# Talking-heads attention with a squared-ReLU MLP on one core: two A v pairs and up to two sets of transposes in every other heavy step

## Chip, cores and metric

One core of one Trainium2 chip runs the whole program. The metric is device time in microseconds (us): the median of three runs of the kernel before was 918.96 us (918.96 to 919.45).

## The reference

The inputs are q, k, v of 4 batches x 12 heads x 448 rows x 64, two 12 x 12 head mixes, and an MLP of 768 x 2048 x 768 over the 1792 rows that attention gives.

```python
scores = scale * np.matmul(q, k.transpose(0, 1, 3, 2))
scores = np.einsum('bhij,hg->bgij', scores, w_pre)
attn = np.exp(scores - np.max(scores, axis=-1, keepdims=True))
attn = attn / (np.sum(attn, axis=-1, keepdims=True) + 1e-09)
attn = np.einsum('bhij,hg->bgij', attn, w_post)
x = np.matmul(attn, v)            # then (B*S, H*D)
h = np.maximum(x @ w_in, 0.0)
out = (s * (h * h) + b) @ w_out
```

## The kernel before

**Tiling.** Each batch's 448 query rows are cut into four chunks of 110, 110, 110 and 118 rows (16 chunks, `chunks`), and each chunk into blocks of up to 10 rows (180 blocks, `blocks`). A block with its 12 heads fills 120 partitions, so a head mix is one matrix product with a 120 x 120 weight. fp32 values are carried as a high part and a remainder ("low part"), and a product is three matmuls: low x high, high x low, high x high.

**Steps.** The loop over `s` is a software pipeline, one block a step. In step s TensorE does `premix(s)` (M: 3 matmuls to `pm`, L612) and `postmix(s-3)` (P: 12 f16 matmuls from `eh` to `po`, L660). VectorE does the row maximum of block s (L619), the reciprocal (L636), the remainder of `eh` of block s-1 (`remainder`, L645) and the copy of `po` into A of block s-4 (`evacuate`, L676). ScalarE does exp (L624) and the f16 high part (`normalize`, L638). GpSimd makes the high and low parts of block s+2 (`split`, L597 and L598), SyncE's queue loads block s+5 from S (`relayout`, L589).

**Work beside the blocks.** Later chunks are prepared in the same steps. Per chunk, `prep_q` makes two sets of transposes of q (4 head pairs and 2 head pairs, L478), `qk_pair` six products q k into a two-bank PSUM tile `sc` (6 matmuls each, L503; ScalarE copies it to S, L513), and `av_pair` six products A v (8 matmuls in the code, 16 rows in the trace, L531). A new batch needs six sets of transposes of k besides (`prep_k`, 4 transposes each, L458). A set lies in a tile of the tag `sc`, of which there is one buffer, and only its first bank is used. ScalarE copies the high part out (L462, L482), and VectorE makes the low part from PSUM and that copy (L239). The low part is put on a list, `later`, and issued by the next `low_parts()`. A q k product behind a set therefore waits for that set's low part twice over: as data or because the tile `sc` must be free.

**What sets the order.** Which step does what is a table, `plan`, made before the loop (L699 to L800): `visits(ci)` names six steps for the q k pairs of a chunk, `prep_q`, `prep_k` and their loads get steps by hand, and the A v pairs get two of the q k steps each. `run_plan(s, True)` issues the loads, `run_plan(s, False)` the rest behind `postmix`. In steps listed in `ahead`, premix, postmix and one set of transposes are issued ahead of the element-wise work. A loop joins two A v pairs into one step only where a transposition stands in the step before (`behind`); elsewhere the pairs stay in steps of their own. In `full` (steps with a q k pair whose predecessor has none) `low_parts()` and `evacuate` come behind the softmax.

**End of attention.** From step 165 (`tail - XA`) on, the first batch's x is split for the MLP: `split_x` has ScalarE copy the high part, and `low_parts` VectorE subtract (L239, both inputs in SBUF), one of six in each of the steps 166 to 171. The MLP's matmuls (L254, L311) follow from about 455 us on.

```python
        low_parts()
        if (s in full or (s >= tail + 4 and s % 2 == 0)) and 0 <= s - 4 < NB:
            evacuate(s - 4)
        if 0 <= s - 1 < NB:
            remainder(s - 1)
        run_plan(s, True)
        if 0 <= s - 3 < NB and s not in ahead:
            postmix(s - 3)
        run_plan(s, False)
```

Of the kernel before, what the change touches and what calls it, by code (L numbers as in the profile page):

```python
# [21 lines left out]
def talking_heads_attention__then__act_relu2_kernel(  # L22
# [427 lines left out]

    def prep_k(b, p):
        low_parts()
        nat = nat_t.pop((b, p))
        tr = bank(f"trk_{b}_{p}") if b == 0 else ps.tile([P, 2, 512], F32, tag="sc", name=f"trk_{b}_{p}")[:, 0]

        for c in (NC - 1, *range(NC - 1)):
            j0 = c * P if b == 0 else min(c * P, S - P)
            nc.tensor.transpose(  # L458
                tr[:, j0:j0 + P], nat[:, c].rearrange("p h d -> p (h d)"), ident
            )  # L460
        t = qkp.tile([P, 2, S], F32R, tag="Tk", name=f"Tk_{b}_{p}", bufs=8)
        nc.scalar.activation(t[:, 0, :], tr[:, :S], AF.Copy)  # L462
        later.append((t[:, 1, :], tr[:, :S], t[:, 0, :]))
        k_t[b, p] = t

    def prep_q(ci, half):

        b, n0, n = chunks[ci]
        low_parts()
# [5 lines left out]
        tr = bank(f"trq_{ci}_{ps_[0]}") if ci < 2 else ps.tile([P, 2, 512], F32, tag="sc", name=f"trq_{ci}_{half}")[:, 0]  # L475
# [226 lines left out]
    fill = []  # L702
    for ci in range(2, NCH):
        b, _, _ = chunks[ci]
        w0 = first[ci - 1] - LD
        news = chunks[ci - 1][0] != b
        back = w0 - (first[ci - 2] - LD)
        if news:
            starts = (w0 - back + 6, w0 - back + 2)
        else:  # L710
            starts = (w0 - back + (10 if back == 12 else 8), w0 + 4)
        for half, step in enumerate(starts):
            at(step, 1, prep_q, ci, half)
            load[step] = 0.375
        if ci > 2:
            at(min(starts) - 8, 0, load_q, ci)
        for p, step in enumerate(visits(ci)):
            if news:
                t = w0 - back + 8 if p == 0 else w0 + 2 * p - 2
                at(t, 1, prep_k, b, p)  # L720
                load[t] = 0.6
                at(t - 4, 0, load_k, b, p)
            at(step, 3, qk_pair, ci, p)
            load[step] = load.get(step, 0) + QK_COST
    ahead = {}
    for ci in range(NCH):
        b = chunks[ci][0]
        w0 = first[ci + 1] + 4
        if ci < NCH - 2:
# [3 lines left out]
            behind = {x[0] + 1 for x in plan if x[3] in (prep_q, prep_k)}  # L733
            for i in range(0, NP, 2):
                if steps[i] not in behind or steps[i + 1] not in behind:
                    j = i if steps[i] in behind or steps[i + 1] not in behind else i + 1
                    steps[i] = steps[i + 1] = steps[j]
                    for n, x in enumerate(plan):
                        if x[0] == steps[j] - 1 and x[3] in (prep_q, prep_k):
                            plan[n] = (-1, *x[1:])  # L740
                            ahead[steps[j]] = x[3:]
# [49 lines left out]
    plan = [x for x in plan if x[0] >= 0]  # L791
# [77 lines left out]
    for s in range(NB + 4):  # L869
# [16 lines left out]
        if 0 <= s - 1 < NB:  # L886
            ops = 7 * NU_EARLY
            due = ops * (s - CONV0) / (tail - LD - 2 * NP - CONV0)
            if s - 1 in mixes:
                for spare in (0, 2):  # L890
                    if turn["ops"] + spare < due:
                        turn["ops"] += convert_step(NU_EARLY)
            if s in ahead:
                premix(s)
                postmix(s - 3)
                f, args = ahead[s]
                f(*args)
            normalize(s - 1)
# [9 lines left out]
        low_parts()  # L908
# [4 lines left out]
        if 0 <= s - 1 < NB:  # L913
            remainder(s - 1)
        run_plan(s, True)
# [124 lines left out]
```

## Time and profile before

| what | value |
|---|---|
| median of three runs | 918.96 us |
| profiled execution: its time, its span | 918.51 us, 916.8 us |
| TensorE busy | 905.5 us (99%) |
| VectorE busy | 652.1 us (71%) |
| ScalarE busy | 562.4 us (61%) |
| GpSimd busy | 394.5 us (43%) |
| mean granted TensorE clock | 0.999 |
| chain that ended last, TensorE's share | 90% |

The profile's page gives busy time by engine (above) and the chain that ended last. The time line of TensorE then gives, from the start of one group of matmuls to the start of the next, what each group costs in its surroundings; a group's own printed length overlaps the next one's, since matmuls are pipelined. The steps can be counted by the premix rows, L612.

### The profile page before, as it was taken

The page shows a single profiled execution, that of the slowest core. Times are in us where ns is not written, and L with a number is a line of the kernel's source. Part 1 is how long each engine was busy: PE and PEld are TensorE (multiplying, and loading weights), DVE is VectorE, ACT ScalarE, POOL GpSimd, SP SyncE. Part 2 cuts the span into 40 slices and gives each one's busy share as a digit, 9 for nine tenths or more (in the row PEclk, how much of TensorE's full clock was granted, in tenths as well). Part 3 has the DMA queues.
Part 4 walks back from the last instruction along what each step waited for, and adds up shares of the span by engine and source line. Part 5 has one row for each costly group of instructions (what it writes and reads, how often), then busy time and mean ns, then how long its engine had stood idle before and what let it go on. Part 6 is the DMA issues. An engine that isn't in the chain of part 4 may idle for free.

```text
span 916.8 us, 19938 instructions
## 1 busy us (share of the span) xinstructions
PE 905.5 (99%) x7538; PEld 784.0 (86%) x7538; DVE 652.1 (71%) x1370; ACT 562.4 (61%) x1260; POOL 394.5 (43%) x454
## 2 busy tenths in 40 slices
PE   8999999999999999999999999999999999999998
PEld 4677777777777777777899999999999999999998
DVE  5889988988989988889796079939107915977111
ACT  5888888888888888887587876021127688600000
POOL 4976677766767677677242333000003333300000
PEclk9999999999999999999999999999999999999999
DMA  5665557564566645546124132344411420345321
GB/s 144 184 158 152 154 136 180 153 158 127 152 162 161 166 127 143 154 131 209 52 68 150 40 95 87 104 156 155 138 44 35 147 78 18 87 155 189 130 95 53
DMA packets 126557, 115.24 MB, mean 126 GB/s; under 512 B 63960, under 2 KB 122348, under 8 KB 126460
## 3 DMA queue, kind: packets, MB, share of 16 engines
q1 hardware_dynamic: 116934, 102.28, 39.7%
q10 hardware_dynamic: 9366, 11.59, 3.5%
q8 instruction: 60, 0.98, 0.4%
q14 instruction: 37, 0.30, 0.1%
q0 software_dynamic: 160, 0.09, 0.1%
HBM read 58.87 MB, written 16.52 MB: 82 GB/s over the span
## 4 chain that ended last, share of the span: by engine, by line
PE 90%; DVE 4%; ACT 3%; DMA 2%; issue 1%; POOL 0%; SPq 0%; ACTq 0%
PE po L311 25%; PE ph L254 24%; PE pm L612 12%; PE po L660 10%; PE xp L531 8%; PE sc L503 7%; DVE st L619 1%; PE ph_head L254 1%; ACT pm L624 1%; PE trk L458 1%; DVE A L676 1%; DMA blk<-S 1%; PE trq L478 1%; ACT S L513 1%; ACT eh L638 1%
## 5 line engine op out<-in xcount | busy, mean ns | idle before, releaser
L311 PE MATMUL po<-w,g 128*128 128x384 f32 x1344 | 233.5, 336 | 0.0
L311 PEld LDWEIGHTS po<-w,g 128*128 128x128 f32 x1344 | 233.0, 188 | 0.3 <-ACT ob L318 0.3
L598 POOL TENSOR_TENSOR hl<-blk,hl 120x448 fp32r<-120x448 f32 (+1 forms) x179 | 204.9, 1145 | 14.9
L272 POOL TENSOR_TENSOR g<-h,g 128x448 fp32r<-128x448 f32 x64 | 79.6, 1244 | 278.9 <-ACT g L271 259.3
L254 PE MATMUL ph<-x,w 128*128 128x448 f32 x810 | 164.1, 362 | 0.0
L254 PEld LDWEIGHTS ph<-x,w 128*128 128x128 f32 x810 | 151.9, 188 | 10.2
L660 PEld LDWEIGHTS <-eh 120*128 120x128 f16 (+1 forms) x2160 | 115.2, 98 | 41.7 <-issue 34.5
L597 POOL TENSOR_SCALAR hl<-blk 120x448 fp32r<-120x448 f32 (+1 forms) x179 | 102.9, 575 | 101.8 <-PE pm L612 93.4
L660 PE MATMUL po<-wpost,eh 120*128 120x120 f16 (+1 forms) x2160 | 144.7, 217 | 0.8 <-DVE A L676 0.4
L645 DVE SCALAR_TENSOR_TENSOR eh<-pm,st,eh 120x448 f16<-120x448 f32 x180 | 122.3, 679 | 18.0 <-ACT eh L638 15.4
L638 ACT ACTIVATE eh<-pm,st 120x448 f16<-120x448 f32 x180 | 114.1, 634 | 14.3 <-DVE st L636 13.8
L619 DVE TENSOR_REDUCE st<-pm 120x1 f32<-120x448 f32 x180 | 110.3, 613 | 11.9 <-PE pm L612 11.1
L624 ACT ACTIVATE pm<-pm,st 120x448 f32<-120x448 f32 x180 | 109.6, 609 | 9.3 <-DVE st L619 7.6
L676 DVE COPY A<-po 128x480 f32<-128x480 f32 x174 | 111.6, 641 | 0.1
L513 ACT ACTIVATE S<-sc 110x896 f32<-110x896 f32 (+1 forms) x91 | 83.5, 917 | 40.2 <-PE sc L503 31.9
L612 PE MATMUL pm<-hl,wpre_hi 120*120 120x448 f32 x360 | 102.4, 366 | 0.7 <-POOL hl L598 0.3
L531 PE MATMUL xp<-A,v 128*64 128x110 f32 (+1 forms) x1536 | 87.1, 263 | 0.0
L503 PE MATMUL sc<-Tk,Tq 64*110 64x448 f32 (+1 forms) x576 | 82.5, 391 | 2.9 <-DVE Tq L239 1.1
L612 PE MATMUL pm<-hl,wpre_lo 120*120 120x448 f32 x180 | 82.8, 460 | 1.6 <-DVE st L636 1.6
L531 PEld LDWEIGHTS xp<-A,v 128*64 128x64 f32 x1536 | 74.0, 137 | 7.3 <-issue 1.3
L318 ACT ACTIVATE ob<-po 128x384 f32<-128x384 f32 x28 | 13.8, 493 | 98.0 <-PE po L311 84.3
L612 PEld LDWEIGHTS pm<-hl,wpre_hi 120*120 120x120 f32 x360 | 64.9, 182 | 6.8 <-POOL hl L598 1.7
(83 smaller groups left out, 970.9 us busy)
## 6 DMA issues: line engine op xcount, KB each, us to landing
blk<-S SPq DMA_DIRECT2D x172, 210.0 KB
raw<-in_moe_w_in_dram SPq DMA_DIRECT2D x32, 384.0 KB
raw<-in_moe_w_out_dram SPq DMA_DIRECT2D x32, 384.0 KB
xraw<-xd SPq DMA_DIRECT2D x48, 224.0 KB
part<-ob ACTq DMA_DIRECT2D x28, 192.0 KB
acc<-part SPq DMA_DIRECT2D x28, 192.0 KB
out_dram<-acc ACTq DMA_DIRECT2D x28, 192.0 KB
v<-in_v_dram SPq DMA_DIRECT2D x24, 192.0 KB
```

Source lines behind the costliest of these rows:

```text
L254: nc.tensor.matmul(ph[:, :S], w[:, i, c0:c0 + P], x[:, y, :], start=(kc == 0 and m == 0), stop=(kc == NKC - 1 and m == 2),)
L311: nc.tensor.matmul(po[:, :NO], g[:, x, c0:c0 + P], w[:, y, :], start=(f == 0 and m == 0), stop=(f == NF - 1 and m == 2),)
L503: nc.tensor.matmul(sc[e][:n, :S], qt[r0:r0 + D, p, x, :n], kt[r0:r0 + D, y, :], start=(m == 0), stop=(m == 2),)
L531: nc.tensor.matmul(xp[e * D:(e + 1) * D, p % 4, :n], vt[:, e, c, :], a[:, c, 2 * p + e, :n], start=(c == 0), stop=(c == NC - 1),)
L598: eng.tensor_tensor(out=hl[:n, 1, :], in0=blk[:n], in1=hl[:n, 0, :].bitcast(F32), op=ALU.subtract)
L612: nc.tensor.matmul(pm[:n, :S], w[:n, :n], hl[:n, x, :], start=(m == 0), stop=(m == 2))
L619: nc.vector.tensor_reduce(out=st[:n, 0:1], in_=pm[:n, :S], axis=AX.X, op=ALU.max, negate=True)
L624: nc.scalar.activation(e[:n], e[:n], AF.Exp, bias=st[:n, 0:1], accum_out=pm[:n, S:S + 1])
L638: nc.scalar.activation(eh[:n, 0, :], e[:n], AF.Copy, scale=st[:n, 3:4])
L645: nc.vector.scalar_tensor_tensor(out=eh[:n, 1, :], in0=e[:n], scalar=st[:n, 3:4], in1=eh[:n, 0, :], op0=ALU.mult, op1=ALU.subtract,)
L660: nc.tensor.matmul(po[:, c * BP:(c + 1) * BP], eh[:n, x, j0:j0 + P], wpost[:n, y].rearrange("p g i -> p (g i)"), start=(m == 0), stop=(m = ...
L676: nc.vector.tensor_copy(dst, src)
```

## The change

In `plan`, for chunks 2 to 15, the A v pairs always come two and two (`steps[p - p % 2]`), and the sets of transposes move to the steps that have them, up to two sets a step (`ahead` now holds a list). The two sets of a step share the two banks of one `sc` tile (`tr_bank`). q k alone stands in the visits between. `prep_k` and `prep_q` of later chunks no longer begin with `low_parts()`. The loads of k keep to 3 to 7 steps ahead of their transposes (before: 4). In the loop, `low_parts()` behind the softmax is kept only up to step 166, and one is added behind `remainder`.

```diff
+    def tr_bank(name):
+        if x_t.get("at") != state["step"]:
+            x_t["at"] = state["step"]
+            x_t["tr"] = ps.tile([P, 2, 512], F32, tag="sc", name=name)
+            return x_t["tr"][:, 0]
+        return x_t["tr"][:, 1]
+
     def prep_k(b, p):
-        low_parts()
+        if b == 0:
+            low_parts()
         nat = nat_t.pop((b, p))
-        tr = bank(f"trk_{b}_{p}") if b == 0 else ps.tile([P, 2, 512], F32, tag="sc", name=f"trk_{b}_{p}")[:, 0]
+        tr = bank(f"trk_{b}_{p}") if b == 0 else tr_bank(f"trk_{b}_{p}")
...
-            steps = [x for x in visits(ci + 2) if x >= w0] + [x for x in after if x < first[ci + 2] + 4]
...
-        news = chunks[ci - 1][0] != b
-        back = w0 - (first[ci - 2] - LD)
...
+        vis = visits(ci)
+        for p, step in enumerate(vis):
             at(step, 3, qk_pair, ci, p)
             load[step] = load.get(step, 0) + QK_COST
-    ahead = {}
+        if ci < 4:
+            for half, step in enumerate(((3, 10), (14, vis[2]))[ci - 2]):
+                if step == vis[2]:
+                    ahead.setdefault(step, []).append((prep_q, (ci, half)))
+                else:
+                    at(step, 1, prep_q, ci, half)
...
+        prev = visits(ci - 1)
+        if chunks[ci - 1][0] != b:
+            when = prev[4], vis[0], vis[0], vis[2], vis[4], vis[4]
+            for p, step in enumerate(when):
+                at((prev[4] - 4, vis[0] - 4, vis[0] - 3, vis[0] - 1, vis[0] + 1, vis[0] + 3)[p], 0, load_k, b, p)
+                ahead.setdefault(step, []).append((prep_k, (b, p)))
+            step = prev[2]
+        elif chunks[ci - 2][0] != b:
+            step = vis[0]
+        else:
+            step = prev[4]
+        ahead.setdefault(step, []).append((prep_q, (ci, 0)))
+        ahead.setdefault(vis[2], []).append((prep_q, (ci, 1)))
+        at(step - 8, 0, load_q, ci)
...
-            behind = {x[0] + 1 for x in plan if x[3] in (prep_q, prep_k)}
-            for i in range(0, NP, 2):
-                if steps[i] not in behind or steps[i + 1] not in behind:
...
+            steps = [steps[p - p % 2] for p in range(NP)]
...
-                f, args = ahead[s]
-                f(*args)
+                for f, args in ahead[s]:
+                    f(*args)
...
-        low_parts()
+        if s <= tail - XA + 1:
+            low_parts()
...
             remainder(s - 1)
+        low_parts()
         run_plan(s, True)
```

TensorE, steps 74 to 76 (the premix `pm` names the step; `trk_2_1` is a set of transposes of k for batch 2, pair 1; `xp` an A v pair, `sc` a q k pair; of the 24 rows of each postmix the first two are shown). Before:

```order
L612 MATMUL pm_74_3581<-hl_74_3491,wpre_hi_125 120x448 x2
...
L531 MATMUL xp_5_0_3463<-A_5_2921,v_2_838 64x110 x8
L503 MATMUL sc_8_0_3614<-Tk_2_0_3447,Tq_8_3164 110x448 x6
L612 MATMUL pm_75_3636<-hl_75_3533,wpre_lo_126 120x448
L612 MATMUL pm_75_3636<-hl_75_3533,wpre_hi_125 120x448 x2
...
L458 MATMUL trk_2_2_3665<-ident_124,nk_2_2_3459 128x128 x4
L612 MATMUL pm_76_3680<-hl_76_3575,wpre_lo_126 120x448
```

and with the change:

```order
L621 MATMUL pm_74_3558<-hl_74_3479,wpre_hi_125 120x448 x2
...
L466 MATMUL trk_2_1_3575<-ident_124,nk_2_1_3390 128x128 x4
L466 MATMUL trk_2_1_3575<-ident_124,nk_2_2_3447 128x128 x4
L540 MATMUL xp_5_0_3451<-A_5_2912,v_2_835 64x110 x8
L540 MATMUL xp_5_0_3451<-A_5_2912,v_3_910 64x110 x8
L512 MATMUL sc_8_0_3616<-Tk_2_0_3435,Tq_8_3253 110x448 x6
L621 MATMUL pm_75_3637<-hl_75_3520,wpre_lo_126 120x448
```

Two sets and two A v pairs now precede the q k pair of step 74, and step 75 keeps premix and postmix alone.

VectorE in the same place (`st` the row maximum and reciprocal, `Tk` a low part of k, `A` the copy of `po`, `eh` the remainder, `u`, `w` the conversion of MLP weights). Before:

```order
L619 TENSOR_REDUCE st_74_3585<-pm_74_3581 120x1
L239 TENSOR_TENSOR Tk_2_1_3571<-trk_2_1_3566,Tk_2_1_3571 128x448
L676 COPY A_6_3405<-po_70_3553 128x48x10
L645 SCALAR_TENSOR_TENSOR eh_73_3579<-pm_73_3540,st_73_3544,eh_73_3579 120x448
L158 TENSOR_SCALAR u_3_3629<-raw_3_2656 128x384
L636 RECIPROCAL st_74_3585<-st_74_3585 120x1
```

and with the change:

```order
L628 TENSOR_REDUCE st_74_3591<-pm_74_3558 120x1
L239 TENSOR_TENSOR Tk_2_1_3580<-trk_2_1_3575,Tk_2_1_3580 128x448
L239 TENSOR_TENSOR Tk_2_2_3586<-trk_2_1_3575,Tk_2_2_3586 128x448
L685 COPY A_6_3394<-po_70_3540 128x48x10
L654 SCALAR_TENSOR_TENSOR eh_73_3589<-pm_73_3527,st_73_3531,eh_73_3589 120x448
L181 SCALAR_TENSOR_TENSOR w_2_2996<-raw_2_2001,u_2_2998 128x384
```

Both low parts stand between the row maximum and the copy of the step in which their transposes are.

VectorE in steps 166 and 167 (`x_0_0_0`, `x_0_0_1` are low parts of x). Before:

```order
L619 TENSOR_REDUCE st_166_7630<-pm_166_7626 120x1
L239 TENSOR_TENSOR x_0_0_0_7614<-xraw_0_0_0_7523,x_0_0_0_7614 128x448
L645 SCALAR_TENSOR_TENSOR eh_165_7623<-pm_165_7588,st_165_7592,eh_165_7623 120x448
L636 RECIPROCAL st_166_7630<-st_166_7630 120x1
L676 COPY A_14_7367<-po_163_7636 128x48x10
L619 TENSOR_REDUCE st_167_7664<-pm_167_7660 120x1
L239 TENSOR_TENSOR x_0_0_1_7649<-xraw_0_0_1_7525,x_0_0_1_7649 128x448
L645 SCALAR_TENSOR_TENSOR eh_166_7657<-pm_166_7626,st_166_7630,eh_166_7657 120x448
```

and with the change:

```order
L628 TENSOR_REDUCE st_166_7618<-pm_166_7614 120x1
L239 TENSOR_TENSOR x_0_0_0_7602<-xraw_0_0_0_7511,x_0_0_0_7602 128x448
L654 SCALAR_TENSOR_TENSOR eh_165_7611<-pm_165_7576,st_165_7580,eh_165_7611 120x448
L645 RECIPROCAL st_166_7618<-st_166_7618 120x1
L685 COPY A_14_7355<-po_163_7624 128x48x10
L628 TENSOR_REDUCE st_167_7652<-pm_167_7648 120x1
L654 SCALAR_TENSOR_TENSOR eh_166_7645<-pm_166_7614,st_166_7618,eh_166_7645 120x448
L239 TENSOR_TENSOR x_0_0_1_7637<-xraw_0_0_1_7513,x_0_0_1_7637 128x448
```

The low part of step 166 keeps its place; the five of steps 167 to 171 change places with the remainder.

The steps whose content changes are 14 to 41, 63 to 86 and 108 to 131. In them 24 A v pairs that had a step of their own before form 12 double ones, and 12 steps have two sets of transposes (six of k and k, three of k and q, three of q and q).

## Rows read from the trace of the kernel before

**Rows 1.** Windows (length, busy by engine, PEclk, DMA share): three stretches that change, one that doesn't.

```profile
49.36:118.24 68.88, 68.56 (x808) 53.24 (x806) 62.73 (x138) 57.78 (x147) 48.85 (x60) 1.00 0.57 152
166.23:226.63 60.40, 59.65 (x702) 46.19 (x699) 54.90 (x121) 49.81 (x128) 42.35 (x50) 1.00 0.54 145
274.24:334.71 60.47, 60.15 (x703) 46.27 (x700) 55.17 (x122) 50.45 (x128) 42.75 (x51) 1.00 0.54 147
226.63:274.24 47.61, 47.61 (x556) 36.53 (x554) 41.31 (x90) 40.41 (x103) 33.57 (x40) 1.00 0.60 157
```

**Rows 2.** Time line of PE, steps 73 and 74: start, length, engine, line, operation, tiles.

```profile
193.37 0.61 PE L458 MATMUL trk<-ident,nk 128*128 128x128 f32 x4
193.73 0.45 PE L612 MATMUL pm<-hl,wpre_lo 120*120 120x448 f32 x1
...
194.43 0.81 PE L660 MATMUL po<-wpost,eh 120*128 120x120 f16 x12
195.16 0.97 PE L531 MATMUL xp<-A,v 128*64 128x110 f32 x16
196.07 0.85 PE L503 MATMUL sc<-Tk,Tq 64*110 64x448 f32 x6
```

**Rows 3.** Time line of PE, step 71, which has a set and two A v pairs.

```profile
186.13 0.81 PE L660 MATMUL po<-wpost,eh 120*128 120x120 f16 x12
186.77 0.61 PE L458 MATMUL trk<-ident,nk 128*128 128x128 f32 x4
187.31 1.73 PE L531 MATMUL xp<-A,v 128*64 128x110 f32 x32
188.97 0.87 PE L503 MATMUL sc<-Tk,Tq 64*118 64x448 f32 x6
```

**Rows 4.** Time line of PE: first and last of 24 single A v pairs ahead of q k.

```profile
69.06 0.97 PE L531 MATMUL xp<-A,v 128*64 128x110 f32 x16
70.18 0.87 PE L503 MATMUL sc<-Tk,Tq 64*118 64x448 f32 x6
...
327.82 0.97 PE L531 MATMUL xp<-A,v 128*64 128x110 f32 x16
328.73 0.86 PE L503 MATMUL sc<-Tk,Tq 64*110 64x448 f32 x6
```

**Rows 5.** Time line of PEld, steps 108 and 110: first and last of three such waits.

```profile
274.64 0.28 PEld L612 LDWEIGHTS pm<-hl,wpre_hi 120*120 120x120 f32 x2 [0.24 <-POOL hl L598]
...
278.63 0.28 PEld L612 LDWEIGHTS pm<-hl,wpre_hi 120*120 120x120 f32 x2 [0.24 <-POOL hl L598]
```

**Rows 6.** Time line of PE in the prologue: eight transposes in a row.

```profile
8.54 1.09 PE L458 MATMUL trk<-ident,A_k 128*128 128x128 f32 x8
9.56 0.87 PE L503 MATMUL sc<-Tk,Tq 64*110 64x448 f32 x6
```

**Rows 7.** Time lines of ACT and DVE, step 71: high copy and low part.

```profile
187.42 0.54 ACT L462 ACTIVATE Tk<-trk 128x448 fp32r<-128x448 f32 x1 [0.67 <-PE trk L458]
187.99 0.62 DVE L239 TENSOR_TENSOR Tk<-trk,Tk 128x448 fp32r<-128x448 f32 x1 [0.53 <-ACT Tk L462]
```

**Rows 8.** Time lines of DVE, POOL and PE in steps 166 to 168.

```profile
414.64 1.35 DVE L239 TENSOR_TENSOR x<-xraw,x 128x448 fp32r<-128x448 f32 x1
417.66 0.61 DVE L239 TENSOR_TENSOR x<-xraw,x 128x448 fp32r<-128x448 f32 x1
414.38 1.14 POOL L598 TENSOR_TENSOR hl<-blk,hl 120x448 fp32r<-120x448 f32 x1
416.73 0.44 PE L612 MATMUL pm<-hl,wpre_lo 120*120 120x448 f32 x1 [1.60 <-DVE st L636]
```

**Rows 9.** Time lines of SP's queue (load of k, pair 2) and PE (start of step 29).

```profile
80.53 2.67 SPq L408 DMA_DIRECT2D nk<-in_k_dram  x2
83.25 0.60 SPq L411 DMA_DIRECT2D nk<-in_k_dram  x1
85.37 0.45 PE L612 MATMUL pm<-hl,wpre_lo 120*120 120x448 f32 x1
```

More of the change, by code (lines that the diff above doesn't have):

```diff
@@ L468, in prep_q @@
         b, n0, n = chunks[ci]
-        low_parts()
+        if ci < 2:
+            low_parts()
         nat = nat_t[ci]
@@ L474, in prep_q @@
         ps_ = half if ci == 0 else range(4) if half == 0 else range(4, NP)
-        tr = bank(f"trq_{ci}_{ps_[0]}") if ci < 2 else ps.tile([P, 2, 512], F32, tag="sc", name=f"trq_{ci}_{half}")[:, 0]
+        tr = bank(f"trq_{ci}_{ps_[0]}") if ci < 2 else tr_bank(f"trq_{ci}_{half}")
         tr3 = tr[:, :4 * CH].rearrange("p (a n) -> p a n", a=4)
@@ L700, in visits @@
         return [w0 + i for i in (1, 3, 5, 7, 9, w1 - w0 - 1)]
-    fill = []
+    fill, ahead = [], {}
     for ci in range(2, NCH):
@@ L705, in talking_heads_attention__then__act_relu2_kernel @@
         w0 = first[ci - 1] - LD
-        news = chunks[ci - 1][0] != b
-        back = w0 - (first[ci - 2] - LD)
[L708 to L722, printed above, removed]
+        vis = visits(ci)
+        for p, step in enumerate(vis):
             at(step, 3, qk_pair, ci, p)
             load[step] = load.get(step, 0) + QK_COST
-    ahead = {}
+        if ci < 4:
[4 more added lines that the diff above has]
+                    at(step, 1, prep_q, ci, half)
+            if ci == 3:
+                at(6, 0, load_q, ci)
+            continue
+        prev = visits(ci - 1)
[12 more added lines that the diff above has]
+        at(step - 8, 0, load_q, ci)
     for ci in range(NCH):
@@ L732, in talking_heads_attention__then__act_relu2_kernel @@
             assert len(steps) == NP
-            behind = {x[0] + 1 for x in plan if x[3] in (prep_q, prep_k)}
-            for i in range(0, NP, 2):
-                if steps[i] not in behind or steps[i + 1] not in behind:
[L736 to L741, printed above, removed]
+            steps = [steps[p - p % 2] for p in range(NP)]
             for p, step in enumerate(steps):
@@ L790, in talking_heads_attention__then__act_relu2_kernel @@
     assert not fill
-    plan = [x for x in plan if x[0] >= 0]
     plan.sort(key=lambda x: (x[0], x[1], x[2]))
@@ L907, in talking_heads_attention__then__act_relu2_kernel @@
             softmax(s)
-        low_parts()
+        if s <= tail - XA + 1:
+            low_parts()
         if (s in full or (s >= tail + 4 and s % 2 == 0)) and 0 <= s - 4 < NB:
@@ L914, in talking_heads_attention__then__act_relu2_kernel @@
             remainder(s - 1)
+        low_parts()
         run_plan(s, True)
```

## The prediction

> **What bounds the kernel now.** I read the page first: by its busy times in the table above TensorE is busy 99% of the span, so only time that TensorE itself spends, or waits, can be won. Next the windows by stretch: in the three stretches whose steps change (together 68.88 + 60.40 + 60.47 = 189.75 us) TensorE is idle for hardly 1.4 us, and VectorE is the next engine, busy for 54.90 of 60.40 us (91%) in the second; in the stretch that doesn't change, it is 41.31 of 47.61 (87%) [rows 1]. The granted clock is 1.00 in all of them. The third view is TensorE's time line, read from start to start, because there a wait hides in the distance between two groups: an A v pair reaches its q k pair after 0.91 us in step 74 (195.16 to 196.07) [rows 2], but the first of 24 single pairs takes 1.12 us (69.06 to 70.18) [rows 4]. That is a wait for a low part, of which the idle column shows little. So the questions are how many groups of matmuls become cheaper by standing together, and which waits stay.
>
> **The change part by part.** All sums are against the profiled execution's 918.51 us; the median of the runs is 918.96, so 0.45 is added at the end. A difference of under 0.2% (1.8 us) can't be told from no change by a measurement of this kernel.
>
> *Two A v pairs in one step.* A single pair takes 0.91 us when nothing disturbs it (195.16 to 196.07, and 327.82 to 328.73) [rows 2, 4], two in a row 1.66 (187.31 to 188.97) [rows 3]. Joining two saves 2 x 0.91 - 1.66 = 0.16, and 24 single pairs become 12 double ones: 12 x 0.16 = **1.9 us less**.
>
> *The waits of q k behind a single pair.* Of the 24 single pairs eleven take 0.90 to 0.91 and thirteen take longer; over all 24 the excess is 2.3 us (the first has 0.21, the last none) [rows 4]. The cause is that one pair is too short to cover the high copy, the low part and the release of the one `sc` tile. Behind two pairs and one set, in step 71, q k starts without a wait [rows 3, 7]. In the change no single pair is left, so **2.3 us go**. Ends: 0 to 2.3.
>
> *The run of light steps.* Steps 106 to 109 are four light ones in a row, and in 108, 109 and 110 the premix waits for the split of GpSimd, 0.24 us on the weight load in the first and the last [rows 5]; as a little of that lies beside matmuls still running I take 0.2 each, 0.6 in all. In the change a double pair stands in step 108 (and in 18 and 63), so that GpSimd gets ahead: **0.6 us less**, ends 0 and 0.6.
>
> *Transposes.* A set of k alone in a light step takes 0.36 us (193.37 to 193.73) [rows 2]. As the first set ahead of A v it takes 0.54 (186.77 to 187.31), and postmix before it is 0.64 instead of 0.73 (186.13 to 186.77 against 194.43 to 195.16) [rows 2, 3], so 0.45 in all: 0.09 more, less some 0.03 that postmix gains where a premix follows it directly. As a second set I take the same pace as alone, 0.36 to 0.40. The nearest row for eight in a row is the prologue's: 1.02 from the first transposition to the q k behind (8.54 to 9.56) [rows 6], against 0.54 + 0.39 = 0.93. In each stretch four sets become first ones that did not stand ahead of A v before: 12 x 0.06 = 0.7, and with the prologue's price for the six steps with two sets of k 0.5 more. I take 0.7: **0.7 us more**; ends 0.5 and 1.2.
>
> *Two low parts ahead of one q k.* This is the wait that the change adds, and no row shows it. In step 71 the high copy starts 0.65 us behind the first transposition, the low part runs from 187.99 to 188.61, and q k starts at 188.97, 0.36 later [rows 7, 3]; as some 0.15 of that is the way from VectorE to TensorE, 0.2 is spare. With a second set q k comes 0.39 later, and the second low part ends at most 0.62 later (its own length, right behind the first). So the wait is 0.62 - 0.39 - 0.2 = 0.03 at VectorE's pace of step 71, and up to 0.62 where VectorE comes late. What is queued behind the two low parts is the copy of `po` and the remainder; the copy is needed by the next step's postmix, which comes after two pairs and a q k pair, over 2 us later, so that is covered. I take 0.05 for each of 12 steps: **0.6 us more**; ends 0 and 12 x 0.62 = 7.4.
>
> *VectorE and ScalarE in all.* No operation is added or removed, so VectorE's 54.90 us must fit into 60.40 - 1.4 = 59.0 us in the second stretch, 93% [rows 1]. It fits, with less room than before.
>
> *The loads of k.* A load takes SyncE's queue 3.3 us to issue [rows 9]. The transposes of pair 2 move from step 30 to step 29, and its load still stands in step 26, now right behind that of pair 1 (before, a step lay between). In the trace its last part is issued by 83.85, and step 29 starts at 85.37 [rows 9]. The second set of step 29 would come 1.8 us into it (premix, postmix, first set: 0.7 + 0.64 + 0.4), less 0.4 for the set that step 28 loses and some 0.5 that the change has gained by then: at 86.3. I cost it at nothing, as the other five loads get as many steps as before or more. How long such a transfer takes to land stands in no row that I have, so the other end is a wait of 1 us in each of three stretches, 3 us.
>
> *Low parts of x behind the remainder.* In step 166 nothing moves: the low part there takes 1.35 us from 414.64 instead of 0.61 as at 417.66, beside a GpSimd subtraction that runs from 414.38 for 1.14, and the premix of step 168 starts 1.6 us late at 416.73 [rows 8]. The five later ones change places with a remainder; TensorE's start-to-start distances in steps 168 to 172 hold no wait, so nothing is won there and I cost it at nothing; the cover is two to three us of matmuls in each of these steps. By the page SBUF — State Buffer of the Trainium skill, section "SBUF: two separate sides", a VectorE instruction with two SBUF inputs and a GpSimd one exclude each other for a whole instruction; the 1.35 beside 0.61 agrees. By that rule each moved low part may meet another GpSimd instruction than before and be up to 0.74 later or earlier, which the sum holds as no change. Ends: the nearest row is the 1.6 us wait, either way.
>
> The sum: -1.9 - 2.3 - 0.6 + 0.7 + 0.6 = -3.5. 918.51 - 3.5 = 915.0, on the median's scale 915.5.
>
> **The rivals.**
>
> *The waits only change their place.* Two joined pairs ease q k, but VectorE at 93% gives its lateness to another: premix waits for the remainder (its `pm` buffer), or postmix for the copy of `po`. For it: the 1.6 us wait of step 168, which is of this kind [rows 8]; against it: the stretch that doesn't change has double pairs already and TensorE is busy there for all of its 47.61 us [rows 1]. Then the cheaper groups alone are left, -1.9 + 0.7 = -1.2: 917.8.
>
> *The second low part decides.* VectorE reaches the two low parts late, because in the three steps since the last heavy one TensorE runs faster than VectorE can follow; q k then waits a whole low part in each of 12 steps. That is 7.4 instead of 0.6: -4.1 + 7.4 = +3.3, 922.3, slower. It turns from gain to loss at 4.1 / 12 = 0.34 us a step. Against it: 0.03 by the working from step 71 and the 9% that VectorE is free. For it: that thirteen of 24 single pairs already wait shows that VectorE has no large lead.
>
> *A load of k lands late.* 3 us of waits take the gain down to 0.5: 918.5. Against it: the queue has issued the load 2.4 us ahead of its use even so.
>
> *The clock falls.* Eight transposes in a row stand in the prologue, and the clock of the whole run is 1.00 in every stretch that I looked at [rows 1, 6], so I leave this one chance in a hundred; no row is at the lower level. If it fell in the 12 steps of about 4.7 us, each would take twice as long: an estimate of +56 us. The page TensorE: Matmul & The Clock Gate of the Trainium skill, section "Part 4: PE-mode transpose", says that the full clock does not engage for transposes; the stretches here, with their sets of transposes, kept 1.00.
>
> **How the numbers follow.** The forecast, waits gone, gets 0.70: between 914.0 (no wait left, nothing for the second low part) and 917.0 (half of the waits stay). Waits that change their place, or a gain that is smaller for another reason, 0.19. The second low part, 0.07. Late loads, 0.03. The clock, 0.01. The range from 913.8 to 917.9 leaves out the slower cases, and a tenth of the others. Faster by over 0.2% (below 917.1): the forecast and a fifth of the second case, 0.74. Within 0.2%: 0.18. Slower: 0.08.
>
> **What would show it.** Right: in the changed kernel's time line the two pairs take 1.66 to 1.77 from start to q k in the steps with two sets as in the others; the windows of the three stretches add up to about 186 us; premix distances of steps 108 to 110 hold no GpSimd wait; VectorE's share in the stretches rises to 93%. Wrong: distances of 2 us and more from A v to q k in steps 29, 33, 37 (the second low part); waits at premix or postmix in the light steps behind a double set (waits that moved); a wait of transposes for a DMA in steps 29, 74 or 119; or a changed length of steps 166 to 172, of which I expect none.

## The result and the profile after

The changed kernel takes 929.92 us (median of four runs, 929.39 to 932.0); the kernel before takes 919.21 beside it (918.96 to 919.98). The ratio is 1.0119, 95% interval 1.0102 to 1.0137: **slower by 10.7 us**, where 915.5 was forecast. The forecast and its whole range were wrong.

The profiled execution took 932.0 us, the longest of the four, with a span of 930.1 against 916.8. The page of the changed kernel, its first part (busy time, share, instructions):

```profile
PE 908.2 (98%) x7538; PEld 784.7 (84%) x7538; DVE 651.5 (70%) x1370; ACT 564.1 (61%) x1260; POOL 394.3 (42%) x454
```

Every engine has as many instructions as before and is busy for nearly as long; TensorE's busy share fell from 99 to 98%. Windows of the changed kernel by the same steps as in [rows 1] (length, busy by engine, PEclk, DMA share, GB/s):

```profile
50.24:122.65 72.41, 69.36 (x809) 53.31 (x807) 61.35 (x134) 58.28 (x147) 48.70 (x60) 1.00 0.53 142
170.25:235.53 65.28, 60.74 (x702) 46.20 (x699) 54.02 (x118) 50.88 (x128) 42.30 (x50) 1.00 0.50 134
283.58:347.02 63.44, 60.16 (x702) 46.12 (x700) 54.03 (x117) 50.57 (x128) 41.93 (x50) 1.00 0.51 137
235.53:283.58 48.05, 47.68 (x556) 36.53 (x554) 42.51 (x96) 40.87 (x104) 34.30 (x41) 1.00 0.62 160
```

The three stretches whose steps change add up to 201.13 us instead of 189.75, 11.4 us more; the fourth has 0.4 more. TensorE's busy time in the three is 190.26, but it is now idle for 10.9 us where it had been idle for 1.4. The clock is 1.00 throughout. The rest of the span's 13.3 us is 0.9 in the prologue, 1.0 behind step 131 and -0.4 between the first two stretches. The first two of these are no more than executions differ by: over the thirteen traces of this case step 14 begins at 49.22 to 50.24 us, and what stands behind step 131 takes 581.5 to 583.6.

Where the idle time lies shows in one step with two sets. Time lines of PE, ACT and DVE of the changed kernel, step 74 (start, length, engine, line, operation, tiles, count, idle time before and what ended it):

```profile
200.24 0.61 PE L466 MATMUL trk<-ident,nk 128*128 128x128 f32 x4
200.44 0.60 DVE L628 TENSOR_REDUCE st<-pm 120x1 f32<-120x448 f32 x1
200.88 0.54 ACT L470 ACTIVATE Tk<-trk 128x448 fp32r<-128x448 f32 x1 [0.56 <-PE trk L466]
201.48 0.66 PE L466 MATMUL trk<-ident,nk 128*128 128x128 f32 x4 [0.63 <-ACT Tk L470]
202.06 1.73 PE L540 MATMUL xp<-A,v 128*64 128x110 f32 x32
202.17 0.54 ACT L470 ACTIVATE Tk<-trk 128x448 fp32r<-128x448 f32 x1 [0.75 <-PE trk L466]
202.75 1.16 DVE L239 TENSOR_TENSOR Tk<-trk,Tk 128x448 fp32r<-128x448 f32 x2 [1.71 <-ACT Tk L470]
203.82 0.65 DVE L685 COPY A<-po 128x480 f32<-128x480 f32 x1
204.05 0.86 PE L512 MATMUL sc<-Tk,Tq 64*110 64x448 f32 x6 [0.26 <-DVE Tk L239]
```

TensorE's four transpositions of the second set begin 1.24 us behind the first four (200.24 to 201.48), right behind ScalarE's copy of the *first* set, although they write another bank. VectorE, which has had its data since that copy, does nothing for 1.71 us and begins the first low part behind the copy of the *second* set. So the first transposition reaches A v after 1.82 us here (0.93 was forecast), and the two pairs reach q k after 1.99 instead of 1.66. The twelve steps with two sets have these distances:

| step with | steps | first transposition to A v, us | two pairs to q k, us |
|---|---|---|---|
| k and k | 6 | 1.83 | 1.98 |
| k and q | 3 | 1.58 | 1.66 |
| q and q | 3 | 1.40 to 1.44 | 1.75 |

The instruction list of the changed kernel gives the reason (the first transposition of each set in step 74, and the two low parts, with what each waits for; `Activation_49` counts what ScalarE has done, the `DMAHW` names count loads):

```
L466 MATMUL trk_2_1_3575<-ident_124,nk_2_1_3390 128x128 [waits DMAHW3_49,Activation_49]
L466 MATMUL trk_2_1_3575<-ident_124,nk_2_2_3447 128x128 [waits DMAHW7_49,Activation_49]
L239 TENSOR_TENSOR Tk_2_1_3580<-trk_2_1_3575,Tk_2_1_3580 128x448 [waits Activation_49]
L239 TENSOR_TENSOR Tk_2_2_3586<-trk_2_1_3575,Tk_2_2_3586 128x448
```

Both sets carry the name of one tile, `trk_2_1`: the two banks of one `sc` allocation. By the counts in the list, the second set waits for ScalarE's copy of the first set, and the first low part for the copy of the second set; the second low part needs no wait of its own behind it. These waits are instructions of the program, put there when it is built. **Theory:** they are made for the whole tile, so that an engine that touches it waits for the last other engine that touched it, whichever bank. **First rival:** VectorE comes late, as the forecast's second rival had it, and the order of the copies makes no difference. Others are named with the runs.

A second, smaller loss appears in steps 65, 66, 100 and 111. Time lines of SP's queue, ACT, PEld and PE of the changed kernel, steps 63 to 66:

```profile
172.24 4.10 SPq L598 DMA_DIRECT2D blk<-S  x3
176.07 0.92 ACT L522 ACTIVATE S<-sc 118x896 f32<-118x896 f32 x1 [2.53 <-DMA blk<-S]
177.04 0.49 PEld L512 LDWEIGHTS sc<-Tk,Tq 64*118 64x118 f32 x6 [0.26 <-ACT S L522]
178.90 0.43 PE L621 MATMUL pm<-hl,wpre_lo 120*120 120x448 f32 x1 [0.97 <-DVE eh L654]
```

ScalarE's copy into S waits for a block load from the buffer that it overwrites, the next q k product for that copy, and the premix of step 66 comes late. Steps 65 and 66 take 1.8 us too long together.

### The profile page after: what moved, and what is told of

Same layout as the page of the kernel before. It is cut to its first block, busy times and chain, and to the rows that moved or that the text cites. A ratio compares the mean times of both kernels' runs of the same rounds, so it can differ in the third digit from the quotient of the medians.

```text
span 930.1 us, 19941 instructions
## 1 busy us (share of the span) xinstructions
PE 908.2 (98%) x7538; PEld 784.7 (84%) x7538; DVE 651.5 (70%) x1370; ACT 564.1 (61%) x1260; POOL 394.3 (42%) x454
## 4 chain that ended last, share of the span: by engine, by line
PE 86%; DVE 5%; ACT 4%; DMA 3%; POOL 1%; issue 1%; SPq 0%; ACTq 0%; POOLq 0%
PE po L311 25%; PE ph L254 24%; PE pm L621 11%; PE po L669 9%; PE xp L540 7%; PE sc L512 6%; DMA blk<-S 3%; PE trk L466 1%; DVE A L685 1%; PE ph_head L254 1%; DVE st L628 1%; ACT pm L633 1%; ACT Tk L470 1%; DVE Tk L239 1%; PE trq L487 1%
## 5 line engine op out<-in xcount | busy, mean ns | idle before, releaser
L272 POOL TENSOR_TENSOR g<-h,g 128x448 fp32r<-128x448 f32 x64 | 79.3, 1240 | 280.6 <-ACT g L271 266.9
L540 PE MATMUL xp<-A,v 128*64 128x110 f32 (+1 forms) x1536 | 84.4, 262 | 0.0
```

What stands on the lines that cost most here:

```text
L540: nc.tensor.matmul(xp[e * D:(e + 1) * D, p % 4, :n], vt[:, e, c, :], a[:, c, 2 * p + e, :n], start=(c == 0), stop=(c == NC - 1),)
```

## The experiments

The kernel before took 918.93 us beside the first four runs, 919.5 beside the next four and 919.01 beside the last three; each ratio is to the one beside it.

**1. All transposes first, both copies behind.** The changed kernel, still with one two-bank tile; `high_part` puts a copy on a list, and `high_parts` issues the list behind the last set, each copy followed by its entry in `later`:

```diff
-        nc.scalar.activation(t[:, 0, :], tr[:, :S], AF.Copy)
-        later.append((t[:, 1, :], tr[:, :S], t[:, 0, :]))
+        high_part(t[:, 0, :], tr[:, :S], t[:, 1, :])
...
                 for f, args in ahead[s]:
                     f(*args)
...
+                high_parts()
```

> The change, but in a step with two sets all transposes are issued first and the two high copies behind them, so that no transposition waits for ScalarE's copy of the other set, which lies in the same two-bank tile. Theory (the shared tile ties the second set to the first set's high copy, 0.75 to 0.88 us in each of 12 steps, and the first low part to the second high copy): the distance from the first transposition to A v falls from 1.83 to about 0.95 us for two sets of k, from 1.58 to 0.75 for k and q, from 1.42 to 0.68 for q and q; since the copies now start later, q k behind the two pairs waits 0.8 us instead of 0.33 with two sets of k, about 0.3 with k and q, 0.1 with q and q. In all some 6 us less than the change: 923.7 us (922.5 to 925.5). Rival (the second set waits for its load from DRAM): the distance stays at 1.83, 929.9 us. Rival (VectorE is the bound of these steps): the distance falls and q k waits the whole of it, 929 to 930 us.

Measured: 924.12 us, ratio 1.0056 (1.0042 to 1.007). Step 74 in this run:

```profile
197.18 1.04 PE L479 MATMUL trk<-ident,nk 128*128 128x128 f32 x8
198.16 1.73 PE L551 MATMUL xp<-A,v 128*64 128x110 f32 x32
198.27 0.98 ACT L461 ACTIVATE Tk<-trk 128x448 fp32r<-128x448 f32 x2 [1.00 <-PE trk L479]
199.28 1.16 DVE L239 TENSOR_TENSOR Tk<-trk,Tk 128x448 fp32r<-128x448 f32 x2 [1.30 <-ACT Tk L461]
200.58 0.88 PE L523 MATMUL sc<-Tk,Tq 64*110 64x448 f32 x6 [0.69 <-DVE Tk L239]
```

Eight transpositions reach A v after 0.98 us. The first copy now starts only behind the last of them, the low parts only behind both copies, and the wait at q k grows to 2.42 - 1.66 = 0.76. In all twelve steps the transpositions reach A v after 0.98, 0.73 and 0.68 by kind, and A v reaches q k after 2.42, 2.00 and 2.01. So the waits of the transpositions, 9.9 us, are gone, and those of q k have grown from 2.2 to 6.6 us: about half of the loss has gone, the rest now stands at the low parts.

**2. The same, with q k of those steps one step later**, so that the low parts have time. These steps also join `full`, so that their low parts come behind the softmax.

```diff
...
+    two = {x for x, sets in ahead.items() if len(sets) > 1}
+    plan = [(x[0] + 1, *x[1:]) if x[3] is qk_pair and x[0] in two else x for x in plan]
```

> As the run before, and the q k pair of each of the 12 steps with two sets stands one step later, behind that step's premix and postmix. Theory: 1.3 us more lie between the two pairs and q k, which is more than the 0.8 us that the low parts are late, so no wait is left in these steps: 12.3 us less than the change, 917.6 us (916.5 to 919). Rival (VectorE is the bound): the lateness turns up at premix or postmix of the light steps, 922 us or more. Rival (loads late): 929 us.

Measured: 935.38 us, ratio 1.0172 (1.0156 to 1.0187): the worst of all. The theory was wrong; the lateness turns up where the rival had it. Steps 29 to 31 of this run:

```profile
88.95 1.16 DVE L239 TENSOR_TENSOR Tk<-trk,Tk 128x448 fp32r<-128x448 f32 x2 [1.56 <-ACT Tk L461]
90.02 0.65 DVE L696 COPY A<-po 128x480 f32<-128x480 f32 x1
90.72 0.80 PE L680 MATMUL po<-wpost,eh 120*128 120x120 f16 x12 [0.38 <-DVE A L696]
91.18 1.47 DVE L175 SCALAR_TENSOR_TENSOR raw<-raw 128x384 uint32<-128x384 uint32 x1
92.57 0.15 DVE L656 RECIPROCAL st<-st 120x1 f32<-120x1 f32 x1
```

VectorE stands still for 1.56 us until both copies are there. Without the q k product behind A v, the next step's postmix comes sooner and waits for VectorE's late copy of `po`, and the lateness runs on through the light steps. The rival's cause is only half borne out: VectorE has no idle time behind the low parts in these steps, but it lost 1.56 us ahead of them by waiting.

**3. The low parts of x alone.** The kernel before, with only this part of the change:

```diff
-        low_parts()
+        if s <= tail - XA + 1:
+            low_parts()
...
+        low_parts()
         run_plan(s, True)
```

> The kernel before with one part of the change alone: the low parts of x of steps 167 to 171 behind the remainder. Theory: no matmul waits there, so no change, 919.2 us (918.7 to 919.7), and steps 166 to 172 keep their lengths within 0.05 us. Rival (the moved low parts meet GpSimd's subtractions and push the copy and row maximum back): up to 1.6 us more, 920.8.

Measured: 919.14 us, ratio 1.0002 (0.9992 to 1.0012): no change, as expected.

**4. Run 2 with the loads of q earlier**, where a batch begins:

```diff
-        at(step - 8, 0, load_q, ci)
+        at(step - (11 if chunks[ci - 1][0] != b else 8), 0, load_q, ci)
```

> As the second run (copies behind both sets, q k a step later), and the load of q for a batch's first chunk three steps earlier, as before the change. In the change's trace it lies behind the loads of v in SyncE's queue and ahead of the block loads of the next steps, and a copy to S in step 65 waits 2.5 us for a block load. Theory: that queue made steps 65 and 66 some 1.6 us longer (and 111 by 0.5), so 1.5 to 2 us less than the second run: 915.9 us (914.8 to 917). Rival (the wait comes from elsewhere): as the second run, 917.6.

Measured: 933.2 us, ratio 1.0161 (1.0143 to 1.0179), by the medians 2.2 less than run 2, though their executions overlap (931.81 to 936.32 against 933.05 to 936.43). Steps 65 and 66 were back at 2.23 and 1.32 us in its trace, while step 63 grew from 3.96 to 4.67. So the late block load is a matter of SyncE's queue.

**5. Run 1 with copy, low part, copy, low part in program order.** If engines take turns on one tile, the second copy must now wait for the first low part. The reciprocal and the row maximum of the step go ahead of these four.

```diff
...
+                    while raised:
+                        hi, x, lo = raised.pop(0)
+                        nc.scalar.activation(hi, x, AF.Copy)
+                        later.append((lo, x, hi))
+                        low_parts()
...
```

> As the first run (copies behind both sets), but in program order each high copy is followed at once by its low part: copy, low part, copy, low part, with row maximum and reciprocal ahead of them on VectorE. Theory (ScalarE and VectorE take turns on one PSUM tile in program order, though the sets lie in different banks): the second copy now waits for the first low part, so the chain grows by one low part less one overlap, q k waits some 1.1 us instead of 0.7 with two sets of k, 0.65 instead of 0.25 with k and q, 0.4 instead of 0.25 with q and q: 4 us more than the first run, 928 us (926.5 to 929.5). Rival (a low part waits only for its own copy, and was late for VectorE's other work): the first low part starts half a us earlier than in the first run, 920.8 us (919.8 to 922.5).

Measured: 927.94 us, ratio 1.0092 (1.0074 to 1.011). The predicted turn-taking, in step 74:

```profile
200.72 0.62 DVE L239 TENSOR_TENSOR Tk<-trk,Tk 128x448 fp32r<-128x448 f32 x1 [0.84 <-ACT Tk L939]
201.38 0.54 ACT L939 ACTIVATE Tk<-trk 128x448 fp32r<-128x448 f32 x1 [0.69 <-DVE Tk L239]
201.95 0.62 DVE L239 TENSOR_TENSOR Tk<-trk,Tk 128x448 fp32r<-128x448 f32 x1 [0.61 <-ACT Tk L939]
```

ScalarE's second copy reads a bank that the first low part doesn't touch, both only read, and still it starts after that low part has ended (200.72 + 0.62 = 201.34). The instruction list agrees: the second copy carries a wait for VectorE, where in the changed kernel it waits for TensorE alone. VectorE was not late here; it waited for ScalarE. This speaks against the first rival and for the tile.

**6. The two sets in two steps.** The first set of each pair moves behind the postmix of the step before, its low part to the head of the heavy step.

```diff
+    for step, sets in ahead.items():
+        if len(sets) > 1:
+            f, args = sets.pop(0)
+            at(step - 1, 1, f, *args)
...
+                low_parts()
                 for f, args in ahead[s]:
                     f(*args)
```

> The change, but of two sets of a step the first goes behind the postmix of the step before, in a tile of its own time, and its low part is issued at the head of the heavy step; A v pairs stay joined. Theory: with one set a tile the 12.3 us of waits in the steps with two sets go and no other comes, as the first set's copy and low part have premix and postmix (1.3 us) before the next set needs the tile: 917.6 us (916.3 to 919), A v to q k at 1.66 to 1.77 in all joined steps. Rival (the second set now waits for the first one's low part): 0.5 to 0.9 us in each of 12 steps, 924 to 928 us.

Measured: 930.31 us, ratio 1.0118 (1.0102 to 1.0134): no better than the change, and dearer than even the rival had it. PE in steps 32 and 33:

```profile
96.50 0.66 PE L466 MATMUL trk<-ident,nk 128*128 128x128 f32 x4 [0.33 <-ACT S L522]
97.61 0.80 PE L669 MATMUL po<-wpost,eh 120*128 120x120 f16 x12
99.03 0.41 PE L487 MATMUL trq<-ident,nq 110*128 110x110 f32 x2 [0.62 <-DVE Tk L239]
```

The sets have tiles of their own, but there is one `sc` buffer: the first set waits for the copy to S of the q k product before it, the second for the first set's low part.

**7. Run 6 with the loads of q as in run 4.**

> As the run before, with the load of q for a batch's first chunk three steps earlier, as before the change. Theory: 2 us less than the run before (that was the difference of the two runs with q k a step later), 915.7 us (914.5 to 917), below the kernel before. Rival (that wait is hidden without the other delays): as the run before.

Measured: 931.59 us, ratio 1.0129 (1.0107 to 1.0152): nothing gained. In its trace steps 65 and 66 got 2.1 us back against run 6, and steps 62 and 63 lost 0.5 of it; steps 170 to 173 took 1.6 longer, and the cause of that stays open.

**8. Run 1 with the loads of q as in run 4.**

> The first run (copies behind both sets) with the load of q for a batch's first chunk three steps earlier. Theory: the waits of steps 65, 66, 100 and 111 go, 1.5 to 2.2 us less than the first run, 922.2 us (921 to 923). Rival: the late block load has another cause, 924.1 us.

Measured: 925.37 us, ratio 1.0063 (1.0047 to 1.0079), not faster than run 1. Steps 65, 66 and 111 got 2.3 us back, but steps 62 and 63 lost 1.22 and 1.04: an earlier load of q only moves the crowding of SyncE's queue.

**9. The change with one-bank tiles.** The decisive run: the same order of work, the same two banks, but each bank a PSUM tile of its own. A q k product then has two tiles, and ScalarE copies it to S with two instructions.

```diff
+    def sc_bank(e, name):
+        return ps.tile([P, 512], F32, tag=f"sc{e}", name=name)
...
-            x_t["tr"] = ps.tile([P, 2, 512], F32, tag="sc", name=name)
-            return x_t["tr"][:, 0]
-        return x_t["tr"][:, 1]
+            return sc_bank(0, name)
+        return sc_bank(1, name)
...
-            x_t["two"] = ps.tile([P, 2, 512], F32, tag="sc", name=f"sc_{ci}_{p}")
-            x_t["sc"] = [x_t["two"][:, 0], x_t["two"][:, 1]]
+            x_t["sc"] = [sc_bank(e, f"sc_{ci}_{p}_{e}") for e in range(2)]
```

> The changed kernel with its two-bank tile divided: the two sets of a step, and the two heads of a q k product, lie in two PSUM tiles of one bank each (the same two banks), so that S is copied by two ScalarE instructions instead of one. Order of the work otherwise as in the changed kernel. Theory (sets in one tile wait for each other's readers because the order is kept tile by tile): the second set no longer waits for the copy of the first, the first low part no longer for the second copy; the first transposition reaches A v in 0.9 to 1.0 us with k and k (1.83 in the changed kernel), two pairs reach q k in 1.66 to 1.8 (1.98), and the 12.3 us of these two waits go: 929.9 - 12.3 = 917.6, with some 0.5 for the longer copies of S 918 (917.3 to 919.5). Rival 1 (the wait comes from ScalarE or from the banks, not from the tile): the second set still starts 1.2 us behind the first, 929 to 931. Rival 2 (two copies of S, about 0.17 us more for each of 91, make ScalarE late everywhere): the waits at the sets go, but others come: 921 or more, and the kernel before with the same division is slower by as much.

Measured: 917.26 us (915.9 to 920.26), ratio 0.9988 (0.9978 to 0.9998), 12.7 below the changed kernel. By the medians it is 1.8 below the one before, by the ratio 1.1, which is hardly more than a measurement of this kernel can tell. Windows of the three stretches, and step 74:

```profile
49.33:117.54 68.21, 68.21 (x809) 53.17 (x807) 61.27 (x134) 58.63 (x162) 48.79 (x60) 1.00 0.57 151
165.26:226.30 61.04, 59.61 (x702) 46.21 (x699) 53.59 (x118) 51.03 (x140) 42.47 (x51) 1.00 0.54 143
274.45:333.36 58.91, 58.91 (x703) 46.04 (x700) 53.56 (x117) 50.83 (x140) 41.96 (x50) 1.00 0.54 146
```

```profile
194.28 1.04 PE L466 MATMUL trk<-ident,nk 128*128 128x128 f32 x8
194.93 0.98 ACT L470 ACTIVATE Tk<-trk 128x448 fp32r<-128x448 f32 x2 [0.56 <-PE trk L466]
195.26 1.73 PE L540 MATMUL xp<-A,v 128*64 128x110 f32 x32
195.50 1.16 DVE L239 TENSOR_TENSOR Tk<-trk,Tk 128x448 fp32r<-128x448 f32 x2 [0.42 <-ACT Tk L470]
196.58 0.65 DVE L685 COPY A<-po 128x480 f32<-128x480 f32 x1
196.91 0.87 PE L511 MATMUL sc<-Tk,Tq 64*110 64x448 f32 x6
```

ScalarE's first copy and VectorE's first low part now run while TensorE and ScalarE are busy with the second set. In this run's instruction list the second set no longer waits for the copy of the first, and each low part carries a wait for its own copy. Transpositions to A v 0.98, A v to q k 1.65, no wait; so in all twelve steps (0.98, 0.73 and 0.68 by kind, 1.66 to q k). The theory's number was 917.6 to 918; both rivals asked for 921 or more.

**10. The kernel before with one-bank tiles**, as a control.

> The kernel before with the same division into one-bank tiles, as a measure of what that costs or gives by itself. Where q k waits for a low part behind a single A v pair nothing changes; the q k product's second head needs the second bank, free earlier; the copies of S end some 0.17 us later. Theory: no change, 918.5 to 920. Rival 2 of the run above: 921 or more.

Measured: 919.48 us, ratio 1.0005 (0.9997 to 1.0014): no change. The division gives the kernel before nothing; what it gave in run 9 came from the steps that two sets share.

**11. Run 9 with two loads of v later.** Behind run 9 the waits of steps 65 and 66 were left (1.7 us). Two of a batch's six loads of v are issued four and five steps later.

```diff
-                    at(step + p % 2, 4, load_v, b + 1, p)
+                    at(step + (4 + p % 2 * 2 if p > 3 else p % 2), 4, load_v, b + 1, p)
```

> As the first run here, with the loads of the next batch's v for pairs 4 and 5 four and five steps later, so that the block loads ahead of steps 65 and 66 are issued without them. Theory (steps 65, 66, 100 and 111 wait 2.3 to 2.6 us in all because the last block load of a chunk stands behind too many other loads on SyncE's queue): these waits go, 2 us less than the first run, about 916. Rival: the load of q and of raw weights alone keep the queue late, or the lateness moves to another step as in the runs with an earlier load of q: 917.5 to 919, no difference.

Measured: 915.92 us (915.05 to 916.26), ratio 0.9963 (0.9951 to 0.9975): **faster than both kernels**, 3.1 us below the one before. The windows of its three stretches:

```profile
50.04:118.73 68.69, 68.43 (x809) 53.18 (x807) 61.36 (x134) 58.73 (x162) 48.83 (x60) 1.00 0.58 152
166.45:225.82 59.37, 59.32 (x702) 46.10 (x700) 53.62 (x118) 51.03 (x140) 41.93 (x50) 1.00 0.55 147
273.97:332.99 59.02, 59.02 (x703) 46.04 (x700) 53.55 (x117) 50.91 (x140) 41.93 (x50) 1.00 0.55 147
```

Steps 65 and 66 are back at 2.23 and 1.35 us, which is the 1.7 us of the second stretch (61.04 to 59.37). The first stretch is 0.5 longer, because a load of k landed late for step 29 in this execution: its last part was issued by 85.63, and the second set waited for it until 87.35.

```profile
87.35 0.65 PE L466 MATMUL trk<-ident,nk 128*128 128x128 f32 x4 [0.26 <-DMA nk<-in_k_dram]
```

Step 100 is still as long as in the changed kernel (1.92 us, 1.49 before); what it takes to shorten it wasn't tried.

## Why the prediction was wrong

**The step that failed** is the transposes' term, forecast at 0.7 us: "As a second set I take the same pace as alone, 0.36 to 0.40." In the change the second set begins 1.24 us behind the first, and the first transposition reaches A v after 1.83, 1.58 and 1.40 to 1.44 us, against 0.98, 0.73 and 0.68 with a tile for each set. That is 6 x 0.85 + 3 x 0.85 + 0.72 + 2 x 0.76 = 9.9 us of waiting that the prediction had at nothing. The row that I leaned on, eight transposes in the prologue [rows 6], is of sets in tiles of their own; that the change's new function hands out two halves of one tile was in the diff, and I described it without asking who waits for what inside that tile. The clue was in the instruction order as well: the second set names the first one's tile.

**Two low parts ahead of one q k.** The mechanism forecast, VectorE's pace, costs nothing: with one-bank tiles two low parts fit behind two pairs without any wait (0.03 each was the working, with 0.15 for the way from VectorE to TensorE; in step 74 of the changed kernel that way takes 0.14, from 203.91 to 204.05). What the change pays, 0.32 in each of six steps and 0.09 in three, 2.2 us, comes from the same tile: the first low part waits for the second copy.

**The rivals.** None named this mechanism. The second low part with its 922.3 stood nearest, and on the right side, but by another cause: VectorE idles in front of the low parts. Waits that change their place cost most in run 2, but the change has some too: in steps 40, 81 and 85 postmix waits for VectorE's copy of `po`, which the prediction held to be covered, and these steps take 0.34, 0.24 and 0.30 us longer than the 1.32 of a light step without a wait. In step 40 of the changed kernel:

```profile
117.71 0.64 PEld L669 LDWEIGHTS <-eh 120*128 120x128 f16 x12 [0.48 <-DVE A L685]
```

Run 9 still has 0.7 of these 0.9 us. The range's slow end, 917.9, left out all of this.

**What was right.** In the three stretches two joined pairs take 1.66 wherever no wait of the shared tile follows them, the 24 single pairs' waits are gone (fourteen of them took longer than 0.91, not thirteen; the excess of 2.3 holds), and so are the waits for GpSimd [rows 5]: the weight loads of steps 108 and 110 now read

```profile
283.65 0.39 PEld L621 LDWEIGHTS pm<-hl,wpre_hi 120*120 120x120 f32 x2
288.86 0.39 PEld L621 LDWEIGHTS pm<-hl,wpre_hi 120*120 120x120 f32 x2
```

The low parts of x are worth nothing (run 3). The clock is 1.00 in all windows, also with eight transposes in a step, so the rule that the prediction cites for the clock showed no effect here. No set of the changed kernel waits for a load of k. The cover is thin, though: where step 29 begins a microsecond or more sooner than in the changed kernel (86.27), runs 1, 8 and 9 have no such wait, but run 5 loses 0.4 us at the second set and run 11 0.5.

**What was missed besides.** I went through the loads of k step by step, but not the loads of q and v, which `plan` moves too. They crowd SyncE's queue ahead of a chunk's last block load, and steps 65, 66 and 111 lose 2.3 us in the stretches, step 100 0.4 outside them. For steps 65 and 66 runs 4 and 11 show that cause; for the other two it is taken to be the same.

**The sum, closed.** With one-bank tiles the stretches take 188.16, of which 1.7 are the waits of steps 65 and 66: 186.5, against 189.75 before, a gain of 3.3 us where the sum over the parts said 3.5 and the prediction named some 186. To that the change adds 9.9 + 2.2 = 12.1 at the shared tile, 2.3 at SyncE's queue and 0.2 more at postmix than run 9: -3.3 + 12.1 + 2.3 + 0.2 = +11.3, and 11.4 was measured. Waits four times as large as the gain stood beside it.

That 3.3 lies so near 3.5 is in part luck. From the kernel before to run 9, start to start in the three stretches, the A v groups fall from 40.69 to 36.46 us, which is the 1.9 + 2.3 forecast; transposes and postmix together rise by 1.3, where 0.7 was forecast; and the low parts cost nothing, where 0.6 was. These two errors cancel.

By the Trainium skill, page Perfetto Trace Analysis, section "Matmuls", independent groups of matmuls should rotate through different PSUM banks, so that one is evacuated while the next is computed. The changed kernel does that for its transposes and gets no overlap; the same banks as two tiles give it. By the page PSUM — Partial Sum Buffer, section "PSUM bank collisions raise a hardware error", accesses of two engines have to be kept apart by bank and 32-partition quadrant; by that rule no wait between two banks is needed, and run 9 has none. Where run 5's two readers took turns they were in two banks, so that turn too came from the tile and not from the rule.

## What to carry to other kernels

Before costing two pieces of work that are put side by side, look up whether they share an allocation. In this program the waits on a PSUM tile are made for the tile, not for the bytes in it, so that the engines fill, copy and read its two halves strictly in turn; the instruction list shows that before anything runs. Two halves that are meant to overlap must be two tiles; here that alone turned +10.7 us into -1.8, by the medians. And a plan that moves loads has to be read queue by queue: the load that suffers is not the one that was moved but the one behind it.

## What was not expected of the hardware

- A copy of S by two instructions of one bank each costs ScalarE hardly more than by one of two banks: 0.98 us for the two together in step 74 of run 9, against 0.92 in the changed kernel, and the same on the mean of all 91; 0.17 more had been expected.
- VectorE's bit instruction of the weight conversion (L175) took 1.47 us in run 2 (91.18 to 92.65). It reads the two halves of one tile and writes one of them in place, and it began beside this row of run 2's GpSimd:

```profile
91.09 1.14 POOL L618 TENSOR_TENSOR hl<-blk,hl 120x448 fp32r<-120x448 f32 x1
```

That is the spread of the low part of x, 1.35 beside a GpSimd subtraction and 0.61 elsewhere [rows 8]. The trace of the kernel before holds more of it. Of its 64 instructions of L175, 59 take 0.55 to 0.56 us; the other five began while a product of two tensors ran on GpSimd (L272), took 1.52 to 1.53, and ended 0.41 to 0.42 behind that product. The other way round, seven products began while an L175 ran: they took 1.40 to 1.56, where those with no VectorE instruction beside them take 1.15 to 1.16. One pair of each kind, GpSimd first and VectorE first:

```profile
538.81 1.16 POOL L272 TENSOR_TENSOR g<-h,g 128x448 fp32r<-128x448 f32 x1 [6.46 <-DMA xraw<-xd]
538.86 1.53 DVE L175 SCALAR_TENSOR_TENSOR raw<-raw 128x384 uint32<-128x384 uint32 x1
491.40 0.55 DVE L175 SCALAR_TENSOR_TENSOR raw<-raw 128x384 uint32<-128x384 uint32 x1
491.45 1.51 POOL L272 TENSOR_TENSOR g<-h,g 128x448 fp32r<-128x448 f32 x1 [2.37 <-ACT g L271]
```

In both kinds the one that starts first keeps its length and the other is drawn out. That the second waits for the first is read from these rows; no run took the GpSimd instruction away.
